# Queuing the transposes of the next expert's rows at the sixth weight block instead of ahead of the first

## The chip, the cores and the metric

The kernel runs on one core of one Trainium2 chip. The core has a matrix engine (TensorE, PE in the profile, with its weight loads as PEld), a vector engine (VectorE, DVE), a scalar engine (ScalarE, ACT), a general engine (GpSimd, POOL) and a queue engine that issues transfers (SyncE, SP). Each engine works through its own list of instructions in the order in which the program wrote it, and engines wait for each other through semaphores. The metric is the time of one execution in microseconds (us); less is better.

## The reference

Windowed attention with sink tokens (4 batches, 8 heads, 768 positions, 64 wide) feeds a first mixture layer, and that feeds a second one, the part that is changed. In the second layer every one of 3072 tokens is given to one of 8 experts, at most 384 tokens each; the assignment takes the best logit first. An expert gathers its 384 rows of 512 numbers, multiplies by a 512 by 1024 matrix, takes the positive part, and multiplies by a 1024 by 512 matrix.

```
logits = x @ w_gate
order = np.argsort(-logits.flatten())
for idx in order:                       # best logit first
    tok, e = idx // E, idx % E
    if assigned[tok] >= 0 or counts[e] >= cap: continue
    assigned[tok] = e; counts[e] += 1
for e in range(E):
    mask = assigned == e
    h = np.maximum(x[mask] @ w1[e], 0.0)
    out[mask] = h @ w2[e]
```

## The kernel before

All stages up to the second mixture layer are left as they are. In the last loop of `attention_mixtures` (line 712) eight experts are worked through, n = 0 to 7, in the order in which the routing fills them. Three kinds of work are interleaved there.

Routing. `step(n+2)` (line 683) finds out which expert fills up next and which 384 tokens it takes. It is one long chain that goes back and forth between DVE and PE: five times DVE compares keys with thresholds (`th`, line 398), PE counts in 24 small matmuls (`rc<-th,ohr`, line 404), DVE compares with the room left (`met`, line 448), PE spreads the answer (`rc<-met,scaleb`, line 450), and DVE forms the next digit (`hit` and `z`, lines 451 and 453); then come two rankings (line 493) and the slot matmuls (`rc<-vt,th`, line 526, 24 of them), out of which DVE makes the list of token numbers `idx` (line 529).

Gathering. `fet(n+2)` (line 686) issues three indirect transfers on POOL (`xg<-x2d,idx`, line 562); each brings 128 rows of 512 numbers. There are six `xg` buffers, so two experts' rows at a time.

Transposes. `trn(n+1)` (line 689) calls `turn` (line 565): for each of four column blocks PE makes three 128 by 128 transposes, one out of each gathered tile, into the one PSUM bank `pt` (line 25, the helper `flip`); ACT copies the bank to a high part `xh` (or `hh`, line 583) and DVE subtracts to get the low part `xl` (or `hl`, line 584). Only then can the next three transposes go into `pt`. Two sets of high and low parts alternate from expert to expert.

Expert. `expert` (line 588) goes through eight weight blocks f = 0 to 7. Per block SP loads two 256 KB tiles (`sa`, `sb`, lines 544 and 545), ACT and POOL or DVE split them into high and low parts (lines 549 and 551), PE makes 12 matmuls of the first layer (`mm`, line 602), ACT and DVE make the high and low part of the positive part (`hh`, `hl`, lines 605 and 606), and PE makes 9 matmuls of the second layer for the block before (`acc`, line 596). At the end the three `acc` banks are copied out and scattered.

The order of the instructions is not written out by hand. A scheduler places them on each engine by a simulated time, by the order in which the program emits them, and by a priority: what stands in `tc.high_priority(offset=k)` competes as if it had been emitted k places earlier. The routing steps stand under an offset of 400 (`s2`), the transposes under one of 100 (`trn_off`, lines 618 and 716). Once placed, the order is fixed: PE waits at an instruction whose data is late, and everything behind it waits too.

The call sites are these:

```
            if n<6:
                with tc.high_priority(offset=s2): S.append(step(n+2)); fet(n+2)
            if n<7:
                with tc.high_priority(offset=trn_off): trn(n+1)
            E.expert(*G[n])
```

Of the kernel before, what the change touches and what calls it, by code (L numbers as in the profile page):

```python
# [22 lines left out]
def f32(ap): return ap.bitcast(FT)  # L23
# [511 lines left out]
class Moe2:  # L535
# [29 lines left out]
    def turn(s,xg,more=None):  # L565
# [19 lines left out]
            X.append((h,l))  # L585
        s.ng+=1
        return X
    def expert(s,X,ev,idx):
        nc=s.nc; F=8
        acc=[s.acc.tile([128,512],FT,name=f"acc{t}") for t in range(3)]  # L590
        H=[None]*F; W=[None]*F
        def second(f):
            for t in range(3):
                n=0
                for a,b in ((0,0),(0,1),(1,0)):
                    nc.tensor.matmul(acc[t],H[f][a][:,t*128:(t+1)*128],W[f][1][b],start=(f==0 and n==0),stop=(f==F-1 and n==2)); n+=1  # L596
        for f in range(F):
            W[f]=s.weights(ev,f)
            ps=s.mm.tile([128,512],FT,name="mm"); n=0
            for k in range(4):  # L600
                for a,b in ((0,0),(0,1),(1,0)):
                    nc.tensor.matmul(ps[:,:384],W[f][0][a][:,k,:],X[k][b],start=(n==0),stop=(n==11)); n+=1  # L602
            h,l=(s.main.tile([128,384],FR,name=n%(4+f%2),bufs=1) for n in ("hh%d","hl%d"))
            with s.tc.high_priority():
                nc.scalar.activation(h,ps[:,:384],AF.Relu)  # L605
                nc.vector.scalar_tensor_tensor(l,ps[:,:384],0.0,f32(h),op0=OP.max,op1=OP.subtract)  # L606
            H[f]=(h,l)
            if f: second(f-1)
        second(F-1)
        for t in range(3):  # L610
            o=s.act.tile([128,512],FT,name="og",bufs=3)
            with s.tc.high_priority():
                nc.scalar.activation(o,acc[t],AF.Copy)
            st=nc.gpsimd.indirect_dma_start(out=s.out,out_offset=bass.IndirectOffsetOnAxis(ap=idx[:,t:t+1],axis=0),in_=o,in_offset=None)
            for q in s.scat: s.tc.declare_no_dep(st.ins,q.ins,reason="other rows")
            s.scat.append(st)

def attention_mixtures(tc,q,k,v,w1,w2,w3,wo,wg,u1,u2,out,off=236,native=8,order='a0 a0 a0 a0 w a1 a1 w w w w w a1 a1 a2',order1='a2 o o o o o o a2 a2',acc='011100000010',back=1,at=(1,0),trn_off=100,s1=300,s2=400,nring=6):
    nc=tc.nc
    PS=bass.MemoryType.PSUM  # L620
    with ExitStack() as ctx:
# [20 lines left out]
        with tc.block(schedule_with_timeline_sim=True):  # L642
# [18 lines left out]
            for g in range(NG):  # L661
# [5 lines left out]
                if g==NG-1:  # L667
                    A.extra.release(); work.release(); ac.release(); psv.release(); pss.release(); psp.release()
                    acc=P("acc",1,space=PS); rc=P("rc",2,space=PS)
# [12 lines left out]
        E=Moe2(tc,u1,u2,x2d,out,wp,act,main,mm,acc,pst,A.ident,nring)  # L682
        def step(n):
            e,t=r.phase(n>0) if n<7 else r.last()
            return r.slots(e,t)
        def fet(n):
            ev=nc.sync.value_load(S[n][1][0:1,0:1],min_val=0,max_val=7)
            G.append([E.fetch(S[n][0],None if n else T7*128),ev,S[n][0]])
        def trn(n):
            G[n][0]=E.turn(G[n][0],None if n else (keep,P7))  # L690
        G=[]; T7=3*NG-3; K7={}
# [20 lines left out]
        for n in range(8):  # L712
            if n<6:
                with tc.high_priority(offset=s2): S.append(step(n+2)); fet(n+2)
            if n<7:
                with tc.high_priority(offset=trn_off): trn(n+1)
            E.expert(*G[n])


_INS = ['q', 'k', 'v', 'moe_w1', 'moe_w2', 'moe_w3', 'moe_w_out', 'moe2_w_gate', 'moe2_w1', 'moe2_w2']  # L720
# [25 lines left out]
```

## Time and profile before

| | us |
|---|---|
| median of three runs | 1063.85 (1062.08 to 1066.35) |
| profiled execution, its own time | 1069.6 |
| its span, first to last instruction | 1067.8 |
| PE busy over the span | 984.4 (92%) |
| DVE busy | 771.6 (72%) |
| ACT busy | 512.0 (48%) |
| POOL busy | 413.4 (39%) |

The expert loop runs from about 680 us to the end. A row of the profile gives a start or a window in us from the start of the span. A busy share says little by itself here; what matters is at which instruction PE stands idle, what it waited for, and at what clock it went on. PE's clock has two levels in the records, 1.2 and 2.4 GHz; the column PEclk is the granted clock as a share of the higher one, so 1.00 is full speed throughout and 0.50 half speed throughout. In the text below, "gather 3" is the set of rows of expert 3, and "block" is one f of an expert.

### The profile page before, as it was taken

The page shows a single profiled execution, that of the slowest core. Times are in us where ns is not written, and L with a number is a line of the kernel's source. Part 1 is how long each engine was busy: PE and PEld are TensorE (multiplying, and loading weights), DVE is VectorE, ACT ScalarE, POOL GpSimd, SP SyncE. Part 2 cuts the span into 40 slices and gives each one's busy share as a digit, 9 for nine tenths or more (in the row PEclk, how much of TensorE's full clock was granted, in tenths as well). Part 3 has the DMA queues.
Part 4 walks back from the last instruction along what each step waited for, and adds up shares of the span by engine and source line. Part 5 has one row for each costly group of instructions (what it writes and reads, how often), then busy time and mean ns, then how long its engine had stood idle before and what let it go on. Part 6 is the DMA issues. An engine that isn't in the chain of part 4 may idle for free. (4 is left out here: it accounts for less than half of the span.)

```text
span 1067.8 us, 18672 instructions
## 1 busy us (share of the span) xinstructions
PE 984.4 (92%) x6682; PEld 895.1 (84%) x6682; DVE 771.6 (72%) x1822; ACT 512.0 (48%) x1166; POOL 413.4 (39%) x355
## 2 busy tenths in 40 slices
PE   5879999999999999999999999798798897989997
PEld 3668889989999999999999989677687776879886
DVE  6789876788888878888875448796786767843330
ACT  5765553676576766666653112323232332333441
POOL 3656636144444444454342001434233423353431
PEclk9899999999999999999999999999799988989999
DMA  6554512132121221122100002424333433354430
GB/s 150 147 149 119 158 42 72 46 104 54 23 75 36 46 66 40 48 62 47 44 25 1 1 1 100 143 89 130 99 99 120 127 92 98 102 173 132 150 117 30
DMA packets 148845, 89.61 MB, mean 84 GB/s; under 512 B 90160, under 2 KB 133680, under 8 KB 148752
## 3 DMA queue, kind: packets, MB, share of 16 engines
q1 hardware_dynamic: 144048, 74.39, 25.1%
q0 software_dynamic: 3840, 12.45, 3.4%
q10 hardware_dynamic: 864, 1.57, 0.4%
q8 instruction: 53, 0.87, 0.3%
q14 instruction: 40, 0.33, 0.1%
HBM read 74.76 MB, written 13.76 MB: 83 GB/s over the span
## 5 line engine op out<-in xcount | busy, mean ns | idle before, releaser
L551 POOL TENSOR_TENSOR wal<-sa,wah 128x512 fp32r<-128x512 f32 x64 | 90.1, 1408 | 221.5 <-ACT wah L549 218.2
L202 POOL TENSOR_TENSOR L<-A_w,H 128x768 fp32r<-128x768 f32 x46 | 87.2, 1895 | 140.2 <-ACT H L201 121.1
L317 PE MATMUL mm<-woh,hh 128*128 128x260 f32 (+1 forms) x288 | 82.9, 291 | 2.0 <-DVE LG L320 1.1
L317 PE MATMUL mm<-woh,hl 128*128 128x260 f32 (+1 forms) x288 | 82.1, 289 | 2.3 <-DVE hl L334 1.2
L317 PE MATMUL mm<-wol,hh 128*128 128x260 f32 (+1 forms) x288 | 82.1, 287 | 0.0
L549 ACT ACTIVATE wah<-sa 128x512 fp32r<-128x512 f32 x64 | 40.4, 631 | 85.9 <-PE mm L602 61.3
L596 PE MATMUL acc<-wbh,hl 128*128 128x512 f32 x192 | 81.4, 424 | 0.0
L596 PE MATMUL acc<-wbl,hh 128*128 128x512 f32 x192 | 80.6, 420 | 0.0
L596 PE MATMUL acc<-wbh,hh 128*128 128x512 f32 x192 | 80.3, 418 | 0.0
L298 DVE TENSOR_TENSOR hm<-mm,hm 128x384 f32<-128x384 f32 x96 | 53.0, 552 | 37.8 <-PE mm L295 36.8
L606 DVE SCALAR_TENSOR_TENSOR hl<-mm,hh 128x384 fp32r<-128x384 f32 x64 | 35.4, 553 | 56.8 <-ACT hh L605 56.2
L549 ACT ACTIVATE wbh<-sb 128x512 fp32r<-128x512 f32 x64 | 40.4, 631 | 71.6 <-PE acc L596 68.0
L551 DVE TENSOR_TENSOR wbl<-sb,wbh 128x512 fp32r<-128x512 f32 x64 | 47.8, 747 | 32.5 <-ACT wbh L549 32.4
L295 PE MATMUL mm<-xh,w0h 128*128 128x384 f32 x192 | 67.5, 351 | 1.8 <-ACT xh L284 1.1
L295 PE MATMUL mm<-xh,w1h 128*128 128x384 f32 x192 | 66.6, 347 | 1.9 <-DVE hm L298 1.2
L295 PE MATMUL mm<-xl,w0h 128*128 128x384 f32 x192 | 66.0, 344 | 0.3 <-DVE xl L285 0.3
L295 PE MATMUL mm<-xh,w2h 128*128 128x384 f32 x192 | 66.0, 344 | 0.3 <-ACT hm L297 0.3
L295 PE MATMUL mm<-xh,w1l 128*128 128x384 f32 x192 | 65.2, 340 | 0.0
L295 PE MATMUL mm<-xh,w2l 128*128 128x384 f32 x192 | 65.1, 339 | 0.0
L295 PE MATMUL mm<-xl,w1h 128*128 128x384 f32 x192 | 65.0, 338 | 0.0
L295 PE MATMUL mm<-xh,w0l 128*128 128x384 f32 x192 | 64.9, 338 | 0.0
L295 PE MATMUL mm<-xl,w2h 128*128 128x384 f32 x192 | 64.8, 338 | 0.0
(334 smaller groups left out, 3157.4 us busy)
## 6 DMA issues: line engine op xcount, KB each, us to landing
sa<-in_moe_w_dram SPq DMA_DIRECT2D x64, 256.0 KB
sb<-in_moe_w_dram SPq DMA_DIRECT2D x64, 256.0 KB
st<-in_moe_w_dram SPq DMA_DIRECT2D x18, 512.0 KB
qn<-in_q_dram SPq DMA_DIRECT2D x60, 96.0 KB
x2d<-xo SPq DMA_DIRECT2D x18, 256.0 KB
kn<-in_k_dram SPq DMA_DIRECT2D x32, 128.0 KB
st<-in_moe_w_out_dram SPq DMA_DIRECT2D x6, 512.0 KB
vn<-in_v_dram SPq DMA_DIRECT2D x24, 128.0 KB
```

Source lines behind the costliest of these rows:

```text
L202: nc.gpsimd.tensor_tensor(L,Af,f32(H),op=OP.subtract)
L295: nc.tensor.matmul(ps[:,:384],s.W[i][a][:,p,f*128:(f+1)*128],X[p][b],start=(n==0),stop=(n==11)); n+=1
L298: else: nc.vector.tensor_tensor(m,ps[:,:384],m,op=OP.max)
L317: nc.tensor.matmul(ps[:,:n],H[f][a][:,t*128:(t+1)*128],s.WO[b][:,f,u,:n],start=(k==0),stop=(k==17)); k+=1
L549: nc.scalar.activation(h,src,AF.Copy)
L551: (nc.vector if s.cv%2==0 else nc.gpsimd).tensor_tensor(l,src,f32(h),op=OP.subtract)
L596: nc.tensor.matmul(acc[t],H[f][a][:,t*128:(t+1)*128],W[f][1][b],start=(f==0 and n==0),stop=(f==F-1 and n==2)); n+=1
L606: nc.vector.scalar_tensor_tensor(l,ps[:,:384],0.0,f32(h),op0=OP.max,op1=OP.subtract)
```

## The change

The call of `trn(n+1)` ahead of `expert` goes, with its priority offset. `expert` gets a function `mid` and calls it when it comes to the sixth weight block (f equal to 5), ahead of that block's weight loads. The same 12 transposes per expert with their copies are emitted, for experts 1 to 7, without any priority of their own. The first transposes, `trn(0)`, stay where they are.

```
-    def expert(s,X,ev,idx):
+    def expert(s,X,ev,idx,mid=None):
+
         nc=s.nc; F=8
...
         for f in range(F):
+            if f==5 and mid is not None: mid()
             W[f]=s.weights(ev,f)
...
             if n<6:
                 with tc.high_priority(offset=s2): S.append(step(n+2)); fet(n+2)
-            if n<7:
-                with tc.high_priority(offset=trn_off): trn(n+1)
-            E.expert(*G[n])
+            E.expert(*G[n],mid=(lambda: trn(n+1)) if n<7 else None)
```

What this does to the order on each engine is not in the diff. Up to the fifth block of expert 1 (n = 1) all lists are the same but for buffer numbers. The following is PE's list in expert 3 of the kernel before, in its second block: `L25` are the transposes of gather 4, `L450` is the next link of the routing chain, `L602` and `L596` are the expert's own matmuls.

```order
L602 MATMUL mm<-hh_10556,wal 128x384
L25 MATMUL pt<-ident,xg 128x128
L602 MATMUL mm<-hh_10564,wah 128x384
L450 LDWEIGHTS scaleb
L450 MATMUL rc<-met,scaleb 128x128
L602 MATMUL mm<-hl_10565,wah 128x384
L602 MATMUL mm<-hh_10564,wal 128x384
L25 MATMUL pt<-ident,xg 128x128
L602 MATMUL mm<-hh_10572,wah 128x384
```

The same gather's first transposes stand in the changed kernel in expert 3 too, but behind its fifth block (the lines of `expert` are two later there, so 596 is 597 and 602 is 604):

```order
L597 MATMUL acc_11227<-wbh,hh_11358 128x512
L597 MATMUL acc_11227<-wbl,hh_11358 128x512
L597 MATMUL acc_11227<-wbh,hl_11359 128x512
L25 MATMUL pt<-ident,xg 128x128 x3
L604 MATMUL mm<-hh_10732,wah 128x384
L604 MATMUL mm<-hl_10733,wah 128x384
```

They moved by more than three blocks, and the link L450 no longer stands behind one of them. The slot matmuls of the step that finds gather 4 stand at the end of expert 2 in both.

In expert 1 the move is small. This is PE's list there before, behind the counting matmuls of the fifth block, with gather 2:

```order
L596 MATMUL acc_9895<-wbl,hh_10028 128x512
L25 MATMUL pt<-ident,xg 128x128
L596 MATMUL acc_9895<-wbh,hl_10029 128x512
L596 MATMUL acc_9896<-wbh,hh_10028 128x512
L450 LDWEIGHTS scaleb
L450 MATMUL rc<-met,scaleb 128x128
L25 MATMUL pt<-ident,xg 128x128
L596 MATMUL acc_9896<-wbl,hh_10028 128x512
L596 MATMUL acc_9896<-wbh,hl_10029 128x512
L596 MATMUL acc_9897<-wbh,hh_10028 128x512
L25 MATMUL pt<-ident,xg 128x128
```

and this is the same stretch in the changed kernel:

```order
L597 MATMUL acc_9863<-wbl,hh_9996 128x512
L597 MATMUL acc_9863<-wbh,hl_9997 128x512
L597 MATMUL acc_9864<-wbh,hh_9996 128x512
L597 MATMUL acc_9864<-wbl,hh_9996 128x512
L450 LDWEIGHTS scaleb
L450 MATMUL rc<-met,scaleb 128x128
L597 MATMUL acc_9864<-wbh,hl_9997 128x512
L597 MATMUL acc_9865<-wbh,hh_9996 128x512
L597 MATMUL acc_9865<-wbl,hh_9996 128x512
L597 MATMUL acc_9865<-wbh,hl_9997 128x512
L25 MATMUL pt<-ident,xg 128x128 x3
```

The three transposes moved behind the block's last second-layer matmul, two matmuls later for the last of them, and together.

The gathers on POOL keep their places among the weight splits (L551) and the scatters (L614) almost unchanged. Before, from gather 4 on:

```order
L562 DMA xg<-x2d,idx 128x512 x3
L551 TENSOR_TENSOR wal<-sa,wah 128x512
L614 DMA out_dram<-og,idx 3072x512 x3
L551 TENSOR_TENSOR wal<-sa,wah 128x512 x5
L562 DMA xg<-x2d,idx 128x512 x3
```

and in the changed kernel:

```order
L562 DMA xg<-x2d,idx 128x512 x3
L616 DMA out_dram<-og,idx 3072x512 x3
L551 TENSOR_TENSOR wal<-sa,wah 128x512 x7
L562 DMA xg<-x2d,idx 128x512 x3
```

Gather 5 comes one weight split later on POOL, and nothing else there moves by more than that.

## Rows read from the trace of the kernel before

**Rows 1.** Busy by window: window, width, PE, PEld, DVE, ACT, POOL, clock, DMA, GB/s

```profile
680.00:960.00 280.00, 243.75 (x1838) 204.11 (x1838) 206.63 (x618) 87.89 (x164) 100.03 (x77) 0.91 0.37 113
960.00:1040.00 80.00, 80.00 (x407) 72.05 (x406) 25.47 (x42) 35.22 (x66) 29.89 (x25) 1.00 0.44 138
```

**Rows 2.** Waits of PE from 680 us: total us, times, longest

```profile
PE pt L25 <- DMA xg<-x2d,idx: 23.7, 15, 5.1
PE rc L404 <- DVE th L398: 3.5, 2, 2.9
PE rc L493 <- DVE t1b L472: 3.4, 3, 1.7
...
PE pt L25 <- DVE xl L584: 0.4, 1, 0.4
```

**Rows 3.** Windows around the first transposes of gathers 2 to 6

```profile
763.80:771.20 7.40, 2.83 (x10) 1.49 (x10) 2.96 (x8) 0.00 (x0) 1.30 (x2) 0.67 0.72 246
809.20:815.10 5.90, 2.18 (x10) 1.30 (x10) 1.93 (x5) 0.63 (x1) 2.22 (x2) 0.91 0.65 200
850.70:856.30 5.60, 0.52 (x3) 0.40 (x2) 0.06 (x1) 0.00 (x0) 4.16 (x4) 0.89 0.94 322
895.40:902.00 6.60, 1.59 (x8) 1.11 (x8) 3.23 (x8) 0.00 (x0) 1.96 (x3) 0.80 0.83 272
938.70:945.30 6.60, 2.95 (x35) 2.21 (x35) 2.17 (x6) 0.39 (x1) 5.50 (x5) 0.88 0.80 235
```

**Rows 4.** Timeline of PE at gather 4: start, us, instruction, idle before it

```profile
855.84 0.47 PE L25 MATMUL pt<-ident,xg 128*128 128x128 f32 x1 [5.08 <-DMA xg<-x2d,idx]
...
856.44 0.33 PE L450 MATMUL rc<-met,scaleb 128*128 128x128 bf16 x1
...
858.17 0.52 PE L602 MATMUL mm<-hh,wal 128*128 128x384 f32 x1
```

**Rows 5.** Timeline of DVE at gather 4

```profile
856.81 0.29 DVE L451 TENSOR_SCALAR_CACHE_REDUCE hit<-rc 128x127 bf16<-128x127 f32 x1 [6.06 <-PE rc L450]
...
857.43 1.76 DVE L398 TENSOR_TENSOR th<-z,thr 128x3072 bf16<-128x3072 bf16 x1
```

**Rows 6.** Windows of 10 us behind the waits for gathers 3 to 6, and behind 748.1

```profile
815.10:825.10 10.00, 9.96 (x88) 8.83 (x88) 7.03 (x19) 3.59 (x7) 1.27 (x1) 0.88 0.22 61
856.30:866.30 10.00, 10.00 (x61) 8.38 (x60) 6.14 (x14) 3.12 (x6) 1.27 (x1) 0.72 0.11 32
902.00:912.00 10.00, 10.00 (x82) 7.82 (x81) 4.91 (x12) 4.88 (x10) 4.63 (x4) 0.79 0.35 115
945.30:955.30 10.00, 10.00 (x41) 8.53 (x40) 2.74 (x5) 3.55 (x8) 3.53 (x3) 0.73 0.43 127
...
748.30:758.30 10.00, 10.00 (x65) 8.75 (x66) 9.29 (x36) 2.66 (x5) 2.76 (x2) 0.83 0.26 79
```

**Rows 7.** Chain that ended last, one block at full clock: start, us, what

```profile
999.13 2.08 PE mm L602 x12
1001.21 2.09 PE acc L596 x9
```

**Rows 8.** Timeline of PE, slot matmuls of gather 3 and its third tile's first transpose

```profile
802.29 0.75 PE L526 MATMUL rc<-vt,th 128*128 128x6 bf16 x24 [0.29 <-DVE vt L522]
...
814.62 0.47 PE L25 MATMUL pt<-ident,xg 128*128 128x128 f32 x1 [0.74 <-DMA xg<-x2d,idx]
```

**Rows 9.** Instructions on tile pt from 640 us: durations ns min/median/max

```profile
L583 ACT ACTIVATE xh<-pt x13: 484/492/493, 682.1 to 957.0; 128x384 fp32r<-128x384 f32 x13
L584 DVE TENSOR_TENSOR xl<-pt,xh x13: 543/552/558, 682.6 to 957.5; 128x384 fp32r<-128x384 f32 x13
```

**Rows 10.** Timeline of all engines at gather 5's issue

```profile
892.90 0.95 DVE L428 COPY ohr<-oh 128x3072 bf16<-128x3072 bf16 x1
...
893.09 2.37 POOL L562 DMA_INDIRECT xg<-x2d,idx  x1 [3.12 <-DVE dig L430]
...
895.76 0.95 POOL L562 DMA_INDIRECT xg<-x2d,idx  x1 [0.30 <-issue]
```

More of the change, by code (lines that the diff above doesn't have):

```diff
@@ L616, in expert, with attention_mixtures @@
             s.scat.append(st)
-def attention_mixtures(tc,q,k,v,w1,w2,w3,wo,wg,u1,u2,out,off=236,native=8,order='a0 a0 a0 a0 w a1 a1 w w w w w a1 a1 a2',order1='a2 o o o o o o a2 a2',acc='011100000010',back=1,at=(1,0),trn_off=100,s1=300,s2=400,nring=6):
+def attention_mixtures(tc,q,k,v,w1,w2,w3,wo,wg,u1,u2,out,off=236,native=8,order='a0 a0 a0 a0 w a1 a1 w w w w w a1 a1 a2',order1='a2 o o o o o o a2 a2',acc='011100000010',back=1,at=(1,0),s1=300,s2=400,nring=6):
     nc=tc.nc
```

## The prediction

> **What bounds the kernel now.** I read the windows first. From 680 to 960 us, experts 0 to 4 and the start of 5, PE is busy for 243.75 of 280 us at a mean clock of 0.91; from 960 to 1040 us, where no routing is left, it is busy for all 80 us at 1.00 [rows 1]. So the last part is bound by PE at full speed and can't be helped by a new order, and the first part has 36 us of idle PE and a clock that is 9% short. No other engine is full there: DVE is the next with 206.63 of 280 us.
>
> The view of waits then says what PE stood for: 23.7 us in 15 waits for a gather to land, at the transposes [rows 2]. The routing, which one might suspect first, makes PE wait much less; its largest entries are 3.5 and 3.4 us.
>
> The windows around the first transposes put these waits in their places: idle time is the width less the busy time of PE. Gather 2: 7.40 − 2.83 = 4.57. Gather 3: 5.90 − 2.18 = 3.72. Gather 4: 5.60 − 0.52 = 5.08. Gather 5: 6.60 − 1.59 = 5.01. Gather 6: 6.60 − 2.95 = 3.65 [rows 3]. Together 22.0; what is left of the 23.7, 1.7 us, is gather 1's, and gather 7 has none.
>
> Two things make such a wait dearer than its length. The timeline at gather 4 shows one transpose standing for 5.08 us, and L450, a link of the routing chain, coming behind it at 856.44 [rows 4]; DVE had nothing to do for 6.06 us and waited for just that link [rows 5]. So the routing chain stands still with PE and isn't catching up meanwhile: in that window DVE did 0.06 us of work [rows 3]. And PE goes on at the lower clock: in the 10 us behind the waits for gathers 3 to 6 the granted clock is 0.88, 0.72, 0.79 and 0.73, where it is 1.00 in undisturbed work [rows 1, 6].
>
> **The change part by part.** Nothing is removed or added; 12 transposes per expert, with 4 copies on ACT and 4 subtractions on DVE, change their places.
>
> *Gather 1.* The lists are the same up to the fifth block of expert 1: no change.
>
> *Gather 2.* The last transpose of its first column block moves two second-layer matmuls back; nine of these take 2.09 us [rows 7], so 2 × 0.23 = 0.5 us of the wait is covered. The other 4 us stay, since PE reaches the group before the tiles have landed. I take −0.5 (bounds 0 and −1).
>
> *Gathers 3 to 6.* How late does a gather come? For gather 3 the slot matmuls begin at 802.29 and the third tile lets its transpose start at 814.62: 12.3 us [rows 8]. In the changed list of PE there stand between these two points, by the order, 35 first-layer matmuls, 27 second-layer ones and four countings of 24 small matmuls. At full clock 12 of the first kind take 2.08 us and 9 of the second 2.09 [rows 7]: 35 × 0.173 + 27 × 0.232 = 12.3 us, and the four countings come on top, so the transposes come later than the rows do, if only by the countings. For gather 4 four blocks and more stand between (over 17 us by the same rows), for 5, 6 and 7 as much. These four waits should go: 3.72 + 5.08 + 5.01 + 3.65 = 17.5 us.
>
> *The clock behind them.* A window of 10 us at clock c did (1 − c) × 10 us less work than at full speed: 1.2 + 2.8 + 2.1 + 2.7 = 8.8 us [rows 6]. Without the stall there is nothing in these places that would lower it, so I count all of it (bounds 0 and −8.8).
>
> *What is late next.* The routing chain. During the four waits DVE did 1.93 + 0.06 + 3.23 + 2.17 = 7.4 us of work [rows 3] that PE did not have to wait for, because it stood anyway. What of that was on the chain comes back as waits of PE at L404, L450, L493 or L526, at most all of it; part of it were the experts' own subtractions, which nobody waited for. I take the half, +3.7 (bounds 0 and +7.4, and with new dips of the clock some 5 more).
>
> *The transposes among themselves.* They share one PSUM bank. A group of three can start when ACT (0.49 us) and DVE (0.55 us) have emptied it [rows 9], 1.04 us and the hand-over between engines. The shortest distance in the changed list is 2 first-layer and 4 second-layer matmuls, 1.27 us by rows 7. The one wait of this kind before cost 0.4 us [rows 2]. Some two or three of that size: +1.0 (bounds 0 and +5).
>
> *What else moves.* Gather 5 on POOL comes one weight split later, and it is wanted five blocks later: nothing. The weight loads on SP keep their order, and they are ahead of PE: the view of [rows 2] lists no wait of PE for weights. ACT no longer stands before a copy whose transposes are stuck, which can only help the loads. The rows of the next expert are ready about a block before they are used instead of several; the last group stands at the latest at the start of the seventh block (at most 1.04 us behind it the bank is empty), and then PE has some 6 us to go.
>
> Here the Trainium skill has a rule against the change. A gather's issue on POOL took 2.37 us beside a 0.95 us copy on DVE, and 0.95 us otherwise [rows 10]. The page "SBUF — State Buffer", section "Who interferes with whom", says that VectorE and GpSimd share a pair of ports under an exclusive lock, so that the second to come is blocked for the whole of the other's instruction, and it counts copies and casts in their fast mode among those that take it. With the stalls gone DVE's work lies denser, and if each of a gather's three issues lost those 1.42 us, gather 3 would come 4.3 us later than I count; the trace agrees that single issues are stretched, and shows none where all three are. The sum by the rule would be worse by some 1.5 us, the sum by the row is unchanged.
>
> *Sum.* −17.5 − 8.8 − 0.5 + 3.7 + 1.0 = −22.1 us. Against the profiled execution's own 1069.6 us that is 1047.5. The median of the runs, 1063.85, is 5.7 us below that execution, and the waits are the same work in both; I take the same 22 us off the median: 1042 us.
>
> **The rivals.** *A: the chain takes half back.* The whole 7.4 us come back as waits, and each longer one is followed by a lower clock: behind the wait of 1.7 us for `t1b` [rows 2] the next 10 us ran at 0.83, 1.7 us lost [rows 6]; three of those are 5 us. Gain 22.1 − 3.7 − 5 = 13.4: 1050. For it: the routing was already what PE waited for second. Against: at the waits for gathers 3 to 5 the chain was the one that waited for PE.
>
> *B: the gathers land later still.* The margin of gather 3 is only the four countings. With the work denser the same transfers meet the weight loads; if half of the four waits stay, with their clock, the gain is 9 to 10 us: 1054. Against: gathers 4 to 6 have margins of about 5 us and more.
>
> *C: nothing is won.* The time from one step's slot matmuls to the next would be a length of the chain itself, and PE would wait for it elsewhere: 1063. Against: the 6.06 us in which DVE waited [rows 5]; they can't be part of a chain that has no slack.
>
> *D: slower, by the single bank.* The groups now stand close together in the sixth and seventh blocks, amid the routing. DVE works its list in order, and where a comparison of 1.76 us [rows 5] stands ahead of the subtraction that empties the bank, the next group waits: three gaps in each of experts 2 to 4, nine in all, at up to 1.76 us each, are 16 us, and with the 1.7 us of clock that A counts behind each another 15: 1042 + 31 = 1073. It decides from the point at which the gaps fall below the time of emptying plus one comparison, which most of them do. Against it: before, groups stood as close to comparisons, and PE waited for a subtraction of this kind for 0.4 us in all.
>
> **How the numbers follow.** Forecast 0.62, A 0.18, B 0.05, C 0.08, D 0.07. The likeliest is 1042, its own range 1036 (everything won and nothing given back: 17.5 + 8.8 + 1.0 = 27.3 off 1063.85) to 1048 (7.4 given back and the bank's 1.0 doubled twice over). For 8 in 10 I go from 1034, two us lower for smaller waits for DVE whose dips of the clock go too, to 1055, which takes in A and B and leaves out C and D. About 0.5%, 5.3 us, is what a measurement of this kernel can tell from no change, so faster means below 1058.5: forecast, A and B, 0.85, less a little for their tails, 0.84. Same: C and those tails, 0.09. Slower, above 1069.2: D, 0.07.
>
> **What would show it.** In the profile of the changed kernel: waits of PE at L25 for the gather fall from 23.7 to about 6 us, all of it at gathers 1 and 2; the windows from 800 us on show a clock near 1.00; the wait for L450 behind a stuck transpose is gone from DVE's list. Waits at L404, L450, L493 and L526 together grow by some 4 us. Wrong it would be if the waits for gathers 3 to 6 are still there (B), if waits for DVE grew by 10 us and more (A or C), or if PE waits at L25 for `xl` or `hl` (D).

## The result, and the profile after

The changed kernel takes 1050.7 us (median of 4 runs, 1045.13 to 1053.9), against 1064.24 us for the kernel before on the same chip: a ratio of 0.9857 with a 95% interval of 0.9823 to 0.9891, which is 11.6 to 18.8 us; the medians differ by 13.5. Its profiled execution took 1053.32 us with a span of 1051.5; the one of before had 1067.8.

The windows come first, columns as in [rows 1]: window, width, busy time (and instructions) of PE, PEld, DVE, ACT and POOL, granted clock, DMA share, GB/s. Here of the changed kernel:

```profile
680.00:960.00 280.00, 252.25 (x1919) 214.90 (x1918) 216.92 (x625) 94.46 (x175) 110.27 (x83) 0.96 0.40 123
960.00:1040.00 80.00, 80.00 (x409) 71.50 (x409) 23.86 (x41) 31.22 (x59) 22.71 (x19) 1.00 0.34 103
```

Against [rows 1] PE is busy for 8.5 us more of the same 280, at 0.96 in place of 0.91; the last stretch is as it was. What PE stands for is in its waits from 680 us on (total us, times, longest), the answer to [rows 2]:

```profile
PE rc L450 <- DVE met L448: 9.2, 6, 3.4
PE pt L25 <- DMA xg<-x2d,idx: 6.2, 5, 2.7
PE rc L526 <- DVE vt L522: 5.0, 6, 2.3
PE rc L404 <- DVE th L398: 3.5, 3, 1.9
PE rc L493 <- DVE t1b L472: 2.6, 3, 0.9
PE rc L404 <- DVE ohr L428: 0.5, 1, 0.5
PE pt L25 <- DVE xl L584: 0.3, 1, 0.3
```

Before, the entries of the routing that [rows 2] leave out were these:

```profile
PE rc L526 <- DVE vt L522: 3.3, 4, 2.3
PE rc L450 <- DVE met L448: 2.3, 2, 1.8
PE rc L404 <- DVE ohr L428: 0.9, 3, 0.6
```

The waits for a gather fell from 23.7 to 6.2 us, by 17.5. The waits for the routing's DVE work (lines 404, 450, 493 and 526 together) rose from 13.4 (3.5 + 3.4 and the three above) to 20.8, by 7.4. Most of that is at one link: L450 waits 9.2 us for `met` where it waited 2.3.

Where the rise sits is read from the same view in two parts. Up to gather 2's first transposes (765 us before, 766 after) the lists are the same, and there these waits are 9.8 and 8.9 us. Behind that point, where the order differs, they are 3.7 us before (1.7, 1.0, 0.6 and 0.4; L450 has none) and 11.9 after, so the part that can come from the change is 8.2 us. After, from 766 us on:

```profile
PE rc L450 <- DVE met L448: 5.5, 4, 3.4
...
PE rc L493 <- DVE t1b L472: 2.6, 3, 0.9
PE rc L526 <- DVE vt L522: 2.2, 4, 1.5
PE rc L404 <- DVE th L398: 1.6, 2, 0.8
```

Of the 9.2 us at L450, 1.84 (at 682.09) and 1.89 (at 743.01) stand ahead of that point.

The longest of the new waits, on all engines of the changed kernel (start, us, instruction, idle time before it in brackets):

```profile
888.36 0.34 SPq L545 DMA_DIRECT2D sb<-in_moe_w_dram  x1
...
889.57 0.35 SPq L545 DMA_DIRECT2D sb<-in_moe_w_dram  x1
...
893.24 0.69 DVE L551 TENSOR_TENSOR wbl<-sb,wbh 128x512 fp32r<-128x512 f32 x1 [1.25 <-issue]
...
895.35 0.63 ACT L549 ACTIVATE wbh<-sb 128x512 fp32r<-128x512 f32 x1
895.44 1.27 POOL L551 TENSOR_TENSOR wal<-sa,wah 128x512 fp32r<-128x512 f32 x1 [1.44 <-ACT wah L549]
...
896.01 1.24 DVE L551 TENSOR_TENSOR wbl<-sb,wbh 128x512 fp32r<-128x512 f32 x1 [2.08 <-ACT wbh L549]
...
897.18 0.34 DVE L448 TENSOR_SCALAR met<-rc,roomp 128x128 bf16<-128x128 f32 x1
...
897.57 0.22 PE L450 MATMUL rc<-met,scaleb 128*128 128x128 bf16 x1 [3.38 <-DVE met L448]
```

These lines show a queue. `met` has its data (the count of line 404 ended at 893.45), but stands in DVE's list behind a weight subtraction `wbl`. That one waits 2.08 us for ACT's copy, and then takes 1.24 us beside a subtraction on POOL. ACT's copy of 895.35 began when its load landed; SP issued that load at 889.57, right behind the one of 888.36. SP's own waits from 680 us on say why it came late (queue, line, releaser, total us, times, longest; the longest is the one ahead of 888.36):

```profile
SPq L545 <- DVE wbl L551: 151.2, 34, 12.0
```

A load of `sb` has two buffers and may start only when DVE has subtracted the block before the last. SP waited for DVE's subtractions before too, 161.1 us in all; there the loads of this place were issued from 894.74 us on, while PE stood for gather 5 anyway (895.40 to 902.00, [rows 3]). And the granted clock dips behind the new wait (second row), and not around two short ones, of 0.68 us at 812.82 and 0.81 at 823.81 (first row):

```profile
816.00:826.00 10.00, 9.19 (x102) 7.83 (x100) 7.86 (x20) 2.63 (x5) 2.17 (x2) 1.00 0.19 54
897.57:907.57 10.00, 9.20 (x80) 7.92 (x80) 6.65 (x18) 1.64 (x3) 2.11 (x2) 0.83 0.28 87
```

DVE's `hit`, which in [rows 5] waited 6.06 us for a link stuck behind a transpose, now waits 11.6 us in all 26 places together (25.5 before):

```profile
  PE rc L450: 11.6, 26
```

The loop itself won a little more than the two spans tell. The same instruction at its start, where the lists are still equal, stands here before (first) and after (second):

```profile
680.23 0.22 PE L450 MATMUL rc<-met,scaleb 128*128 128x128 bf16 x1 [1.77 <-DVE met L448]
```

```profile
682.09 0.22 PE L450 MATMUL rc<-met,scaleb 128*128 128x128 bf16 x1 [1.84 <-DVE met L448]
```

So the changed execution entered the loop 1.9 us later, and gained 16.3 + 1.9 = 18.2 us inside. 17.5 − 7.4 = 10.1 of them are waits. The other 8.0 are PE's busy time: from that instruction to the end it fell from 343.74 to 335.72 us for the same 2340 instructions, at a mean clock of 0.96 in place of 0.93 (columns as above, before and after):

```profile
680.23:1067.80 387.57, 343.74 (x2340) 293.58 (x2339) 234.25 (x663) 126.88 (x236) 132.83 (x104) 0.93 0.36 112
```

```profile
682.09:1051.50 369.41, 335.72 (x2340) 288.95 (x2339) 239.24 (x663) 127.04 (x236) 134.67 (x104) 0.96 0.38 118
```

### The profile page after: what moved, and what is told of

Same layout as the page of the kernel before. It is cut to its first block, busy times and chain, and to the rows that moved or that the text cites. A ratio compares the mean times of both kernels' runs of the same rounds, so it can differ in the third digit from the quotient of the medians.

```text
span 1051.5 us, 18670 instructions
## 1 busy us (share of the span) xinstructions
PE 978.9 (93%) x6682; PEld 893.3 (85%) x6682; DVE 774.3 (74%) x1822; ACT 512.4 (49%) x1166; POOL 414.5 (39%) x355
## 5 line engine op out<-in xcount | busy, mean ns | idle before, releaser
L551 POOL TENSOR_TENSOR wal<-sa,wah 128x512 fp32r<-128x512 f32 x64 | 89.1, 1393 | 204.1 <-ACT wah L549 198.3
L597 PE MATMUL acc<-wbl,hh 128*128 128x512 f32 x192 | 78.3, 408 | 0.0
L597 PE MATMUL acc<-wbh,hh 128*128 128x512 f32 x192 | 78.0, 406 | 0.1
L597 PE MATMUL acc<-wbh,hl 128*128 128x512 f32 x192 | 78.0, 406 | 0.0
L551 DVE TENSOR_TENSOR wbl<-sb,wbh 128x512 fp32r<-128x512 f32 x64 | 52.2, 818 | 32.8 <-ACT wbh L549 31.4
```

Of the source, the lines that this page charges most:

```text
L551: (nc.vector if s.cv%2==0 else nc.gpsimd).tensor_tensor(l,src,f32(h),op=OP.subtract)
```

## The experiments

Three theories went in. W: waits for gathers go, with the low clock behind them, and DVE takes part of it back. P: what helps is the lost priority, not the place. C: the routing chain has a length of its own, and nothing can be won by moving transposes. For each run the ratio to the kernel before on the same chip is given with its 95% interval. Waits and spans are those of one profiled execution each.

**Place and priority apart.** First the call back ahead of the first block, but without its priority:

```
-            if f==5 and mid is not None: mid()
+            if f==0 and mid is not None: mid()
```

> The transposes are queued inside the expert ahead of its first weight block: they lose their priority and keep their place in the program. In PE's list gathers 2 to 4 stand as close behind their slot matmuls as before; gathers 5 and 6 stand about a block or two farther off. Theory W (the time falls by the waits for gathers that go, with the low clock behind them, less waits for DVE that come back): PE waits at L25 for about 15 us (1.7 + 4.6 + 3.7 + 5.1), the 8.7 us of gathers 5 and 6 are gone, about 3 us come back for DVE, 5 us of clock are won: 1054. Theory P (the lost priority is what counts, the transposes no longer pushing ahead of the experts' matmuls and the routing): as the changed kernel, 1050.

Measured: 1057.67 us, 0.9933 (0.9912 to 0.9954). Waits for gathers 19.5, the routing's 11.3. That is 4 us above W's time and 8 above P's: gather 6's wait is gone, but of gather 5's 2.2 us are left, and the routing's waits did not grow.

Then the sixth block, but with the old priority:

```
+            if f==5 and mid is not None:
+                with s.tc.high_priority(offset=100): mid()
```

> The transposes are queued at the sixth weight block, as in the changed kernel, but keep their priority offset of 100. In PE's list gathers 2, 3 and 4 stand just where they stood before; 5, 6 and 7 come about one block or more later. Theory W: PE waits at L25 for about 15 us, gathers 5 and 6 wait no longer, about 1054. Theory P: the priority is kept, so nothing is won, 1064. If the place in the program alone made the gain, it would be 1050.

Measured: 1054.81 us, 0.9899 (0.9855 to 0.9943). Waits for gathers 15.3; those of gathers 5 and 6 are gone, those of 2, 3 and 4 remain (4.85, 3.10 and 5.12), and up to there PE's list is the one of before. Time and waits are W's. So each half of the change moves some of the gathers, and each gains. P alone is wrong: the place gains with the priority kept.

**No wait for gathers at all.** The kernel before, with the call of the transposes where it was; for experts 2 to 7 they read a constant tile. Since nothing ties them to the gathers any more, the scheduler places them earlier: those for expert 3 begin at 762.9 us, ahead of the slot matmuls of that step at 795.0, and the order on all engines but SP differs from 738 us on.

```
-            G[n][0]=E.turn(G[n][0],None if n else (keep,P7))
+            G[n][0]=E.turn([io]*3,None,3) if n>1 else E.turn(G[n][0],None if n else (keep,P7))
```

> The kernel before, with the transposes of experts 2 to 7 reading a constant tile instead of the gathered rows, so that no transpose has to wait for a gather; the gathers are still made and not read. What it leaves out: experts 2 to 7 work on wrong rows. Theory W: all 22 us of waits for gathers 2 to 6 go, with 11 us of clock, and some 9 us come back as waits for DVE: 1040, and the waits at L404, L450, L493 and L526 grow from 13 to about 22 us. Theory P: the priority is kept, 1064. Theory C (the routing chain has a length of its own): the waits for DVE grow by the whole 22 us and the time stays above 1058.

Measured: 1040.97 us, 0.9758 (0.9719 to 0.9796). Its waits of PE begin so:

```profile
PE rc L450 <- DVE met L448: 8.2, 5, 3.2
PE rc L526 <- DVE vt L522: 4.7, 4, 2.3
PE rc L493 <- DVE t1b L472: 3.6, 4, 1.0
PE pt L25 <- DMA xg<-x2d,idx: 2.4, 3, 1.7
```

C is wrong: without the waits 22 to 30 us are won, W's 1040 within 1 us. And the give-back appears here too, 20.3 us of waits for the routing, 6.9 more than with the gather waits. So it is not bound to the order of the changed kernel. That it belongs to the loss of the cover alone is not shown, since the order is new here as well.

**One block later.**

```
-            if f==5 and mid is not None: mid()
+            if f==6 and mid is not None: mid()
```

> The changed kernel with the call one weight block later, at the seventh. In PE's list gather 2's transposes then stand three blocks behind their slot matmuls instead of just behind them; gather 1 stays. Theory W: PE's waits at L25 fall from 6.2 to about 1.7 us, with 1.6 us of clock, 2 us come back: 1046, 4 us under the changed kernel. Theory P: no difference to the changed kernel, 1050. Should the rows now come too late for the next expert, PE would wait at the first block of an expert for xh or xl, and the time would be above 1052.

Measured: 1047.99 us, 0.9814 (0.9758 to 0.9871), which the runs don't tell from the change itself. The waits for gathers fall by another 4.6 us, to 1.6, as W had it, and the routing's rise by 3.4, to 24.2, where W had 2. From here on the question was what the give-back is. Theory Q: DVE's links stand behind late weight subtractions. Rival L: the chain is late by its own length.

**One subtraction on POOL.** Of the weight subtractions, one was moved from DVE to POOL; no other instruction of any engine changed its place.

```
-            (nc.vector if s.cv%2==0 else nc.gpsimd).tensor_tensor(...)
+            (nc.vector if s.cv%2==0 and s.cv!=72 else nc.gpsimd).tensor_tensor(...)
```

> The kernel after, with one weight subtraction (line 551, the wbl of the fourth block of the fifth expert) on POOL in place of DVE; every other instruction of every engine keeps its place. In the kernel after it began at 896.01 after a wait of 2.08 us for ACT, took 1.24, and the routing step's met behind it let PE's count of line 450 start at 897.57 after a wait of 3.38 us, the longest of the new waits. Theory Q (the give-back is the chain's DVE links standing in DVE's order behind weight subtractions whose loads are late): the wait falls from 3.38 to under 0.8 us, DVE's waits in all from 20.8 to about 18, time 1048. Rival L (the chain is late by its own length and by the stretched DVE instructions): the wait stays above 2.5 us, time 1050.7. Rival S (the weight blocks themselves are late there, PE has nothing else to do): the wait of line 450 falls, but first-layer products behind it wait 2 to 3 us for wah, wal or wbl, time 1050.7.

Measured: 1051.22 us, 0.9836 (0.9798 to 0.9875); the wait of L450 stayed, at 3.81 us. The experiment missed its aim: it is not the subtraction at 896.01 that had been moved but one further ahead (at 888), so a late one still stood in front of `met`. It tells nothing for or against Q. The next edit (72 replaced by 76) took the right one:

> The kernel after, with one other weight subtraction on POOL: the one that stands in DVE's order right ahead of the met for which PE waited 3.38 us (the subtraction at 896.01); the one moved before stood further ahead, and a late one was left in front of met. Every other instruction keeps its place. Theory Q1 (the link itself is late, behind the subtraction): the wait falls below 0.5 us and PE gains 2.5 to 3.5, time 1048. Theory Q2 (subtraction, link and weight block are late together, because the loads of the weights are issued late from SP's queue): the wait of line 450 falls below 0.5, but the first-layer products behind it wait until their wal is made at about 896.7, so PE gains about 1 us, time 1050. Rival L (the chain's own length): the wait stays above 2.5 us.

Measured: 1052.48 us, 0.9841 (0.9787 to 0.9895). All engines around the link:

```profile
891.58 0.22 PE L450 MATMUL rc<-met,scaleb 128*128 128x128 bf16 x1 [0.24 <-DVE met L448]
...
892.17 4.11 DVE L453 TENSOR_SCALAR z<-w,digit 128x48 bf16<-128x48 f32 x1
...
892.49 1.30 POOL L551 TENSOR_TENSOR wal<-sa,wah 128x512 fp32r<-128x512 f32 x1
...
893.74 1.27 POOL L551 TENSOR_TENSOR wbl<-sb,wbh 128x512 fp32r<-128x512 f32 x1
...
894.97 1.26 POOL L551 TENSOR_TENSOR wal<-sa,wah 128x512 fp32r<-128x512 f32 x1
...
896.31 0.96 DVE L398 TENSOR_TENSOR th<-z,thr 128x1536 bf16<-128x1536 bf16 x1
```

The wait of L450 is 0.24: Q is right on that link. But nothing was won. Two DVE instructions on, the small `z`, which takes 0.25 us elsewhere (887.00 in this run), took 4.11: it ended when the third POOL subtraction in a row did, and PE then waited 3.73 us for `th`. Neither Q1 nor Q2 had this; the wait moved, by another mechanism. The Trainium skill, page "SBUF — State Buffer", section "Who interferes with whom", says that the two engines share a pair of ports under an exclusive lock and that whoever issues first holds it for its instruction. The rows agree that DVE stands while POOL works; that `z` stood through three POOL instructions which all began after it goes beyond the rule, and there the rows decide. The same stretching is in the changed kernel without any edit; twice beside one POOL subtraction:

```profile
810.66 1.29 POOL L551 TENSOR_TENSOR wal<-sa,wah 128x512 fp32r<-128x512 f32 x1
810.74 1.76 DVE L551 TENSOR_TENSOR wbl<-sb,wbh 128x512 fp32r<-128x512 f32 x1 [1.59 <-ACT wbh L549]
...
902.86 1.39 DVE L453 TENSOR_SCALAR z<-w,digit 128x48 bf16<-128x48 f32 x1
902.90 1.30 POOL L551 TENSOR_TENSOR wal<-sa,wah 128x512 fp32r<-128x512 f32 x1 [4.52 <-ACT wah L549]
```

Each stretches the DVE instruction by about 1.1 us (0.69 and 0.25 alone). From 680 to 960 us 22 DVE instructions of the kernel before took over 0.25 us more than the median of their line and form, 18.1 us in all, and 31 of the kernel after, 25.7 us. Every one of them overlaps an instruction on POOL in time.

**Subtractions that wait for nothing.** All second-layer subtractions (the 64 on DVE) read a constant, on the kernel after and on the one before. In this experiment and in the two that follow the scheduler also places other instructions anew, from the loop's start on or earlier, so each changes the order besides what it is meant to change.

```
+            if nm=="wb":
+                c=f32(s.ident)[:,None,:].to_broadcast([128,4,128])
+                nc.vector.tensor_tensor(l.rearrange("p (a b) -> p a b",b=128),c,c,op=OP.subtract)
+            else: nc.gpsimd.tensor_tensor(l,src,f32(h),op=OP.subtract)
```

> The kernel after, with all 64 wb subtractions on DVE, as 62 of them are already, but reading a constant tile in place of the loaded block, so that none waits for a load or for ACT, and no load of sb waits for DVE (the low parts of the second layer's weights are left out of the result). Theory Q: waits of PE for DVE fall from 20.8 to about 13 us (the 3.38 at the fifth expert, and the parts behind late subtractions of the rest), time about 1043. Rival L: they stay at 18 to 21 us, time 1049 to 1051.

> The same edit on the kernel before, where the chain's links lay under the gather waits. Theory Q: waits of PE for DVE 13.4 to about 11, gather waits about 24, time about 1062: so the change is worth about 19 us without late subtractions, against 13 to 15 with them. Rival L: the edit is worth the same on both kernels, so the change is worth 13 to 15 here too.

Measured: on the kernel after 1047.79 us, 0.9779 (0.9721 to 0.9836); on the one before 1058.17, 0.9892 (0.9850 to 0.9934). Waits of the first:

```profile
PE rc L404 <- DVE th L398: 7.0, 9, 0.9
PE rc L526 <- DVE vt L522: 5.8, 6, 3.4
PE pt L25 <- DMA xg<-x2d,idx: 5.8, 5, 2.1
PE rc L493 <- DVE t1b L472: 3.1, 3, 1.3
PE rc L450 <- DVE met L448: 0.8, 1, 0.8
```

L450 falls from 9.2 to 0.8, as Q said. The routing's waits in all fall only from 20.8 to 17.7, since L404 now waits 7.0 for `th` in nine small pieces; this sum and the time lie nearer to L's figures (18 to 21 us, 1049) than to Q's (13, 1043). On the kernel before the edit gained as well, mostly at the gathers (23.7 to 15.0 us), which neither theory had; the change is worth 10.4 us between these two kernels, which the intervals don't tell from what it is worth without the edit. So Q names the place of the longest waits, and is no explanation of the whole sum.

**All subtractions on POOL, at the seventh block.**

```
-            (nc.vector if s.cv%2==0 else nc.gpsimd).tensor_tensor(l,src,f32(h),op=OP.subtract)
+            nc.gpsimd.tensor_tensor(l,src,f32(h),op=OP.subtract)
```

> Call at the seventh block, and all weight subtractions on POOL (some 125 x 1.3 us = 163 us of its 390), DVE keeps only the chain and the small subtractions. Theory Q: gather waits about 2, DVE's waits from 24 to about 15, time about 1041. Rival L: DVE's waits stay at 22 to 24, and POOL's doubled use stretches DVE's instructions, time 1048 to 1052.

Measured: 1068.88 us, 1.0022 (0.9995 to 1.0049): all of the gain is gone, though the gathers wait only 2.0 us. The routing's waits are 34.1, which neither theory had. DVE has fewer instructions, and they take longer:

```profile
762.78 4.45 DVE L453 TENSOR_SCALAR z<-w,digit 128x48 bf16<-128x48 f32 x1
...
763.44 1.29 POOL L551 TENSOR_TENSOR wbl<-sb,wbh 128x512 fp32r<-128x512 f32 x1
764.69 1.28 POOL L551 TENSOR_TENSOR wal<-sa,wah 128x512 fp32r<-128x512 f32 x1
...
765.93 1.25 POOL L551 TENSOR_TENSOR wbl<-sb,wbh 128x512 fp32r<-128x512 f32 x1
...
769.42 0.77 PE L404 MATMUL rc<-th,ohr 128*128 128x128 bf16 x11 [3.88 <-DVE th L398]
```

41 instructions are stretched, by 49.6 us in all (counted as above), each of them beside one on POOL.

**A third buffer for the loads,** on the kernel after, on the one before, and with the call at the seventh block:

```
-... b=s.wp.tile([128,512],FT,name="sb",bufs=2)
+... b=s.wp.tile([128,512],FT,name="sb",bufs=3)
-... l=s.wp.tile(list(src.shape),FR,name=nm+"l",bufs=s.nring)
+... l=s.wp.tile(list(src.shape),FR,name=nm+"l",bufs=s.nring-(nm=="wb"))
```

> The kernel after, with three buffers for the loaded second-layer blocks (sb) in place of two, and five in place of six for their low parts, so that it fits. SP's load of a block then waits for the subtraction of three blocks ago. Nothing is left out of the result. The order of the routing work among the blocks shifts by some places. Q2: SP's wait on DVE's subtractions covers less, no wait of line 450 above 1.5 us, PE's waits for DVE 20.8 falls to 15 to 18, time about 1047. L: 19 to 22 us of waits for DVE, time 1050 to 1052.

> The same buffers on the kernel before. Q2: late loads lay under the gather waits there, so it gains less than on the kernel after: time 1061 to 1064. L: no difference on either.

> Call at the seventh block and three buffers. With the call at the seventh block alone the gather waits were 1.6 and the waits for DVE 24.2. Q2: waits for DVE fall to about 18, time about 1043. L: 22 to 25 us, time 1048.

Measured: 1048.64 us, 0.9795 (0.9740 to 0.9850), on the kernel after; 1067.41, 1.0000 (0.9973 to 1.0028), on the one before; 1042.4, 0.9749 (0.9705 to 0.9794), at the seventh block. On the kernel before the buffer is worth nothing, which Q2 and L both allow. On the kernel after the routing's waits are 18.0 and the longest of L450 is 1.5, Q2's figures, but the gain is not told from none by the intervals. The third beats both kernels of this case: its interval lies below that of the change. It overlaps that of the call at the seventh block alone (0.9758 to 0.9871), so what the buffer adds there is not shown by the times either. Its waits for gathers are 3.0 and the routing's 18.9 (24.2 without the buffer), and its window runs nearly at full clock:

```profile
680.00:960.00 280.00, 257.64 (x2009) 220.49 (x2008) 216.78 (x631) 99.34 (x186) 111.75 (x85) 0.99 0.41 125
```

**All kernels together.** Waits of PE from 680 us on for gathers and for DVE (transposes' copies counted with DVE), and the profiled span:

| kernel | gathers | DVE | sum | span |
|---|---|---|---|---|
| before | 23.7 | 13.8 | 37.5 | 1067.8 |
| all on POOL, seventh block | 2.0 | 34.1 | 36.1 | 1064.3 |
| before, third buffer | 20.8 | 15.2 | 36.0 | 1064.8 |
| first block, no priority | 19.5 | 11.9 | 31.4 | 1053.5 |
| before, free subtractions | 15.0 | 15.3 | 30.3 | 1058.4 |
| sixth block with priority | 15.3 | 12.7 | 28.0 | 1051.0 |
| **after** | 6.2 | 21.1 | 27.3 | 1051.5 |
| seventh block | 1.6 | 24.9 | 26.5 | 1050.8 |
| after, third buffer | 7.0 | 18.7 | 25.7 | 1048.6 |
| after, free subtractions | 5.8 | 18.2 | 24.0 | 1047.8 |
| no gather wait | 2.4 | 21.2 | 23.6 | 1042.3 |
| seventh block, third buffer | 3.0 | 19.2 | 22.2 | 1040.3 |

A straight line through these and the two kernels with one subtraction moved has a slope of 1.65 us of span per us of wait (correlation 0.97, largest miss 3.4 us). So over these kernels a wait went with its own length and some two thirds more. Two limits go with that figure. The kernels differ in order too, and these single executions leave the layer before (its last matmul, line 317) some 5 us apart. And it is no price of every single wait: around the two short ones shown above, of 0.68 and 0.81 us, the clock was 1.00.

## Why the prediction was right, and where it was not

*Gather 1* stayed. *Gather 2*: its cover of 0.5 us did not come. In the changed kernel two transposes waited 4.71 us together, against 4.57 by [rows 3]:

```profile
769.18 0.33 PE L25 MATMUL pt<-ident,xg 128*128 128x128 f32 x1 [2.67 <-DMA xg<-x2d,idx]
771.55 0.48 PE L25 MATMUL pt<-ident,xg 128*128 128x128 f32 x1 [2.04 <-DMA xg<-x2d,idx]
```

*Gathers 3 to 6*: all four waits went, and the sum of waits fell by 17.5, as counted. That they were what mattered agrees with the kernel without gather waits, which is faster still, in an order of its own. Gather 3's margin was no matter of the countings only: from its slot matmuls to its transposes PE took 21 us (803.6 to 824.8), against the 12.3 that the rows needed.

*The clock*: −8.8 was counted, and PE's busy time in the loop fell by 8.0; the line over all kernels agrees (17.5 − 7.4 = 10.1 us of waits, times 0.65, is 6.6). In part the two figures are near each other by luck. Around gather 2 (760 to 800 us) the clock rose from 0.87 to 0.96, which was not counted, and two new dips came, one of them behind 1.55 us for `vt`, the other the one shown above:

```profile
803.61:813.61 10.00, 9.32 (x77) 8.26 (x77) 7.94 (x21) 1.64 (x3) 4.75 (x4) 0.83 0.43 125
```

*The routing chain* is the step that failed in size: "I take the half, +3.7". It was +7.4, so rival A's mechanism with A's size, and with two new dips of 1.7 us each of the 5 us of clock that A adds. A's 1050 is what was measured; it had a chance of 0.18. That 7.4 is also the bound, DVE's work under the four waits, is chance: behind the point where the lists part the rise is 8.2, more than that work. The step reasoned that part of DVE's work under the waits was the experts' own subtractions, "which nobody waited for". The runs show the opposite: a link behind such a subtraction waits for it, in DVE's order. Of the 5.5 us at L450 where the lists differ, 4.6 stand behind one (0.68 at 812.82, 0.51 at 856.29, 3.38 at 897.57); the largest fell to 0.24 when that subtraction left DVE's list. And a link waits beside POOL's subtractions as well. What I weighed of the ports was the wrong victim: the gathers' issues, which did no harm (gathers 3 to 6 are in time), and not DVE's small links. The price was misread too: the issue of [rows 10] lost 1.42 us, more than the 0.95 us copy beside it lasted. How the 7.4 us divide into late subtractions, the ports and the chain's own length stays open; no kernel rid of the gather waits came below 17.7 us of waits for the routing.

*The transposes among themselves*: +1.0 counted, none came; the one wait is 0.3 us where it was 0.4. Rival D is out. B is out, since no wait for gathers 3 to 6 is left, and C by the kernel without gather waits.

*Sum*: −22.1 counted. The steps as measured give −17.5 + 7.4 − 8 − 0.1 = −18.2 in the loop; runs differ by some us ahead of it (1.9 between the two profiled ones), and the ratio of the runs is worth −15.2 (−18.8 to −11.6). So 1050.7 came in place of 1042, inside the range. Of the 8.7 us that are missing, 3.9 are these steps, the routing chain above all. The rest is the step from the profiled executions to the medians (18.2 us in the loop, 13.5 between medians): the prediction took all waits to be the same in both, but the profile of before is of an execution 5.7 us over its median. Which of its waits and dips the median lacks stays open.

## What to carry to other kernels

A wait that is taken away was also a cover: list what the other engines did under it, and whose links stand behind that work in an in-order queue, and count all of it as coming back unless it is shown not to be on a chain. After such a change look at the next resource down the line; here a third load buffer was worth nothing on the kernel before, while the buffer and a call one block later together took the ratio from 0.986 to 0.975 (the later call alone to 0.981). Moving work from DVE to POOL to relieve a chain on DVE can stretch that chain by more than it relieves.

## What the runs showed of the hardware

A DVE instruction of 0.25 us stood for 4.11 and 4.45 us through three POOL subtractions in a row that began after it did, not for one of them only. A wait of PE can cost more than its length: 1.65 us of span per us of wait over these kernels, with the granted clock at 0.83 in the 10 us behind a wait of 3.38 us and at 1.00 around waits of 0.68 and 0.81. And the full clock held in stretches that contain 128 by 128 transposes: it was 1.00 from 960 to 1040 us, where experts 5 and 6 turn the rows of 6 and 7.
